# Measured delays between engines in a list scheduler, and VectorE's on-chip operations placed by GpSimd's ends

## The chip, the cores and the metric

The kernel runs on one core of one Trainium2 chip. A core has a matrix engine (TensorE, PE in the profile), a vector engine (VectorE, DVE), an activation engine (ScalarE, ACT), a general engine (GpSimd, POOL) and a queue engine (SyncE, SP) that issues the DMAs. Each runs its own instruction list in order, and they meet only through semaphores. SBUF is the on-chip memory; PSUM is the small memory that TensorE writes. The metric is device microseconds for the whole program; less is better.

## What is computed

Three blocks in a row: a linear attention with exponential features, a mixture of eight experts whose gates are normalized over rows and columns by turns, and one wide block with a sigmoid gate.

```python
def _attn_ref(q, k, v, omega):           # 4 x 8 heads x 576 tokens x 64, 128 features
    def phi(x):
        h = x @ omega.T - sum(x * x) / 2
        return exp(h - max(h)) / sqrt(m)
    kv = einsum('bhsm,bhsd->bhmd', phi(k), v)
    return (phi(q) @ kv) / (phi(q) @ phi(k).sum() + 1e-6)

def _moe_ref(x, w_gate, w1, w2):         # 2304 tokens x 512, 8 experts of 1024
    P = exp(logits - logits.max())       # then 8 rounds of row and column normalization
    for e in range(8):
        out += P[:, e:e + 1] * (maximum(x @ w1[e], 0) @ w2[e])

def _moe2_ref(x, w_in, w_out):           # 512 -> 2048 -> 512
    h = x @ w_in
    return (h * sigmoid(1.702 * h)) @ w_out
```

## The kernel before

The matrix products are made in float32 precision out of three products of rounded halves (a high part and a low part of each operand), and blocks of four are combined into seven products instead of eight by sums and differences of blocks, so that the other engines form many sums while TensorE multiplies. The 2304 tokens are cut into three groups of 768 (j = 0 to 2). The hidden features are taken two blocks of 256 at a time (c = 0 and 1), which makes 16 pairs for the experts and 4 for the last block. One pair on one token group is a **visit**; there are 60. A visit has an up part (`up_fast`, L1195, 84 matmuls of 384 columns), and a down part (`down_across`, L1349, 84 of 384 columns for the experts; `down`, L1386, 256 columns for the last block). The down part of one visit runs into the up part of the next.

In the up part the PSUM results are combined on VectorE (L1216), gated on VectorE (L1237: relu and gate in one operation), and turned into operands of the down part by `operand`: ScalarE rounds a tile into its high part (L1205, tiles named `h` with c, a number 0 to 6 and 0), and an engine subtracts it for the low part (names ending in 1). Where the source lies in PSUM, VectorE subtracts (L1216). Where it lies in the SBUF tile `ring`, `tt` (L426) records the subtraction at L429 for "VP": either VectorE or GpSimd, as the planner decides. The same helper makes the sums of weight blocks (`raw`), the low parts of the weights (`w1x`, `w2x`, GpSimd alone), sums in `ring`, and at the change from the experts to the last block the operands of the next input out of `acc` (`y_operands`, with high parts at L1046). PSUM results of the down part are added to `acc` on VectorE (L1367, L1412) or copied to another bank by ScalarE (L1361).

The weights of the last block come as 64-bit floats. Between about 440 and 1400 us, 32 pieces are converted (`double_piece`): six VectorE operations each (L1125 to L1141) on the SBUF tile `x2s`, then one on GpSimd (L1149).

Nothing of this is issued in the order of the source. Every operation is recorded in a `Plan` with the engine, a duration, what it reads and writes. `Plan.deadlines` goes back from TensorE's list and gives each operation a latest start; `Plan.run` then plays the program in time: at each moment each free engine takes, of its ready operations, the one with the earliest deadline. "VP" operations lie in a list that VectorE and GpSimd share, and "AV" operations (two PSUM copies of the attention stage, L582 and L689) in one that ScalarE and VectorE share. TensorE's main list is fixed. The order that comes out is the order in which instructions are issued, so the durations and delays in the planner set the order, and the hardware's semaphores the times.

The lines that the change touches are the planner's constants (L33 to L37), `add`, the choice of the next operation in `run` (L134 to L185), the duration formulas (L414 to L424) and `double_piece`.

## Time and profile before

| what | us |
|---|---|
| median of 3 runs (1969.64 to 1972.14) | 1970.06 |
| the profiled execution | 1969.8 |
| its span, first to last instruction | 1968.0 |
| TensorE busy | 1931.8 (98%) |
| VectorE busy | 1483.1 (75%) |
| GpSimd busy | 1265.6 (64%) |
| ScalarE busy | 1044.7 (53%) |
| attention stage, about | 0 to 165 |
| experts, about | 165 to 1600 |
| last block, about | 1600 to 1963 |

A line of a group in the profile reads: source line, engine, operation, tile written and tiles read, shape, count, then busy time, mean duration, and the idle time of its engine just before such instructions with what ended it. In a timeline, a bracket behind a row gives the idle time of that engine ahead of it and the instruction that ended it. Matmuls overlap in the array, so their durations (335 ns) are longer than their spacing; TensorE's pace is read from how many it starts in a stretch of time.

### The profile page before, as it was taken

To read this page: it belongs to the slowest core of one execution; us is meant where nothing else is said; L and a number is where in the kernel's file an instruction comes from. 1 tells how busy PE (TensorE), PEld (TensorE's weight loads), DVE (VectorE), ACT (ScalarE), POOL (GpSimd) and SP (SyncE) were. 2 spreads that over 40 slices of the span, in tenths; PEclk is the share of its full clock that TensorE was granted. 3 is DMA by queue.
4 is the path that set the end of the run, shared out by engine and by line. 5 is a ranking of instruction groups with operands and counts; after the bars stand their busy time and mean duration, and the time that the engine had idled before them with its cause. 6 is when DMAs were issued, how large, how long until landed. Compare 5 with 4: busy or idle time off the path is not lost.

```text
span 1968.0 us, 36376 instructions
## 1 busy us (share of the span) xinstructions
PE 1931.8 (98%) x12899; PEld 1888.0 (96%) x12899; DVE 1483.1 (75%) x2882; ACT 1044.7 (53%) x2393; POOL 1265.6 (64%) x1250
## 2 busy tenths in 40 slices
PE   9999999999999999999999999999999999999998
PEld 7788999999999999999999999999999989999998
DVE  7884377777788788888888797888776785656655
ACT  6885555445445355354445354444545576755653
POOL 5844284866658485766667485757656895847552
PEclk9999999999999999999999999999999999999999
DMA  9867465667677586677676685776676888745653
GB/s 171 215 180 244 151 229 218 224 243 250 230 261 258 214 291 239 232 269 257 221 280 241 220 301 206 253 274 228 235 259 214 293 298 320 264 179 202 238 211 120
DMA packets 259295, 464.07 MB, mean 236 GB/s; under 512 B 75288, under 2 KB 200104, under 8 KB 259112
## 3 DMA queue, kind: packets, MB, share of 16 engines
q1 hardware_dynamic: 259112, 461.74, 67.7%
q8 instruction: 102, 1.67, 0.3%
q14 instruction: 81, 0.66, 0.1%
HBM read 415.45 MB, written 46.21 MB: 235 GB/s over the span
## 4 chain that ended last, share of the span: by engine, by line
PE 78%; DVE 12%; ACT 3%; issue 3%; POOL 2%; DMA 1%; SPq 0%; DVEq 0%; ACTq 0%; POOLq 0%
PE bank L1195 35%; PE bank L1349 29%; PE bank L1386 8%; DVE ring L1216 2%; DVE bank L1237 2%; DVE h L1216 2%; PE bank L598 2%; DVE h L429 2%; DVE bank L1216 1%; ACT acc L637 1%; PE bank L576 1%; POOL h L429 1%; PE pair L704 1%; PE bank L684 1%; PE pair L654 1%
## 5 line engine op out<-in xcount | busy, mean ns | idle before, releaser
L1195 PE MATMUL bank<-xo,w1x 128*128 128x384 f32 x5040 | 913.4, 335 | 1.9 <-ACT ring L1205 1.3
L1195 PEld LDWEIGHTS bank<-xo,w1x 128*128 128x128 f32 x5040 | 875.4, 188 | 5.5 <-ACT bank L1205 2.5
L1349 PE MATMUL bank<-h,w2x 128*128 128x384 f32 x4032 | 734.4, 337 | 7.4 <-ACT bank L1361 3.0
L1349 PEld LDWEIGHTS bank<-h,w2x 128*128 128x128 f32 x4032 | 700.1, 188 | 19.5 <-ACT bank L1361 6.7
L429 POOL TENSOR_TENSOR h<-ring,h 128x384 fp32r<-128x384 f32 x350 | 375.1, 1087 | 152.4 <-ACT h L1205 130.3
L1367 DVE TENSOR_TENSOR acc<-bank,acc 128x384 f32<-128x384 f32 x552 | 282.5, 551 | 141.7 <-PE bank L1349 135.1
L1205 ACT ACTIVATE h<-ring 128x384 fp32r<-128x384 f32 x480 | 239.2, 529 | 152.7 <-DVE ring L1216 143.7
L1205 ACT ACTIVATE ring<-bank 128x384 f32<-128x384 f32 x480 | 235.4, 492 | 148.2 <-PE bank L1195 143.3
L429 POOL TENSOR_TENSOR w1x<-raw,w1x 128x768 fp32r<-128x768 f32 (+1 forms) x120 | 181.2, 1516 | 204.0 <-ACT w1x L1101 203.1
L1205 ACT ACTIVATE bank<-bank 128x384 f32<-128x384 f32 x216 | 103.1, 480 | 386.1 <-PE bank L1195 347.9
L429 POOL TENSOR_TENSOR raw<-raw 128x256 f32<-128x256 f32 x313 | 238.1, 784 | 58.3 <-DMA raw<-in_moe_w_dram 43.0
L1216 DVE TENSOR_TENSOR h<-bank,h 128x384 fp32r<-128x384 f32 x324 | 178.5, 551 | 114.4 <-ACT ring L1205 90.4
L1237 DVE SCALAR_TENSOR_TENSOR bank<-bank,x2s 128x384 f32<-128x384 f32 x336 | 183.9, 558 | 67.6 <-PE bank L1195 66.7
L1216 DVE TENSOR_TENSOR ring<-bank,ring 128x384 f32<-128x384 f32 x432 | 225.7, 547 | 8.5 <-ACT bank L1205 6.3
L429 POOL TENSOR_TENSOR ring<-ring 128x384 f32<-128x384 f32 x111 | 116.0, 1045 | 171.2 <-ACT ring L1205 122.3
L1205 ACT ACTIVATE h<-bank 128x384 fp32r<-128x384 f32 x360 | 176.3, 492 | 53.2 <-DVE bank L1237 38.4
L429 POOL TENSOR_TENSOR w2x<-raw,w2x 128x768 fp32r<-128x768 f32 (+1 forms) x120 | 182.8, 1535 | 23.8 <-ACT w2x L1101 23.3
L1386 PE MATMUL bank<-w2x,h 128*128 128x256 f32 x1512 | 186.6, 281 | 5.7 <-POOL w2x L429 2.4
L1386 PEld LDWEIGHTS bank<-w2x,h 128*128 128x128 f32 x1512 | 183.2, 189 | 8.0 <-POOL w2x L429 2.6
L1216 DVE TENSOR_TENSOR bank<-bank,ring 128x384 f32<-128x384 f32 x240 | 133.4, 558 | 14.2 <-PE bank L1195 12.4
L429 DVE TENSOR_TENSOR h<-ring,h 128x384 fp32r<-128x384 f32 x130 | 121.5, 948 | 4.0 <-ACT h L1205 1.9
L1101 ACT CAST w2x<-raw 128x768 fp32r<-128x768 f32 (+1 forms) x120 | 81.5, 694 | 56.3 <-POOL raw L429 51.4
(132 smaller groups left out, 1307.7 us busy)
## 6 DMA issues: line engine op xcount, KB each, us to landing
xo<-sx SPq DMA_DIRECT2D x413, 768.0 KB, 7.1
raw<-in_moe_w_dram SPq DMA_DIRECT2D x256, 128.0 KB, 4.4
x2s<-scr_g SPq DMA_DIRECT2D x90, 192.0 KB, 6.8
sx<-acc SPq DMA_DIRECT2D x46, 192.0 KB, 3.5
x2s<-in_moe_w_in_dram SPq DMA_DIRECT2D x16, 512.0 KB, 4.6
x2s<-in_moe_w_out_dram SPq DMA_DIRECT2D x16, 512.0 KB, 4.1
sx<-x2s SPq DMA_DIRECT2D x35, 192.0 KB, 3.9
sx<-xo SPq DMA_DIRECT2D x42, 128.0 KB, 2.9
```

The source lines that it names most:

```text
L429: lambda e: e.tensor_tensor(out=out(), in0=a(), in1=b(), op=op), r, w,
L576: nc.tensor.transpose(pt[:, i * P : (i + 1) * P], x[:, 2 * i : 2 * i + 2, :], ident)
L598: nc.tensor.matmul(pj[e][0][:, i * M : (i + 1) * M], xt[r, i * P : (i + 1) * P], om[r, :], start=True, stop=True, skip_group_check=True,)
L637: lambda h=h, pv=pv: nc.scalar.activation(f[:, h, :], pv[:, h // 2, :], AF.Exp, bias=nb[:, h : h + 1], scale=-1.0),
L1101: lambda e, a=a, b=b: nc.scalar.copy(T[w, c, 0][:, a:b], r[:, a:b]), raws, [(w, c, g, 0)],
L1195: nc.tensor.matmul(o(b), T["w1", c, a][:, slot, kk], T["xo"][x][:, y, kk], start=start and kk == 0 and n == 0, stop=kk == 1 and n == 2, sk ...
L1205: rec("ACT", act_us(Q), lambda e: nc.scalar.activation(out(), src(), f, **kw), r, w)
L1216: lambda e: e.tensor_tensor(out=out[0](), in0=a[0](), in1=b[0](), op=op), [a[1], b[1]], [out[1]],
L1237: lambda e: e.scalar_tensor_tensor(out=out[0](), in0=o(b), scalar=0.0, in1=T["G"][th], op0=ALU.max, op1=ALU.mult),
L1349: nc.tensor.matmul(bank[i][:, :Q], T["w2", c, y][:, slot, k * P : (k + 1) * P], T["h", c, a, x], start=s and m == 0, stop=c == 1 and m == ...
L1367: lambda e, i=i, q=q: e.tensor_tensor(out=q, in0=bank[i][:, :Q], in1=q, op=ALU.add), rd + [key], [key],
L1386: nc.tensor.matmul(bank[i][:, u], T["h", c, a, x][:, t * P : (t + 1) * P], T["w2", c, y][:, slot], start=s and m == 0, stop=c == 1 and m = ...
```

## The change

Five things are changed, all in the planner and its numbers.

1. One delay of 0.17 us from any engine to any other becomes a table by pair of engines (0.2 from TensorE to ScalarE or VectorE, 0.163 to TensorE, 0.035 between ScalarE and VectorE, 0.035 to 0.08 with GpSimd). The restart cost for TensorE goes.
2. The time by which an engine can start its next operation ahead of the end of the last becomes a number by engine (0.08, 0.1 and 0.04 us instead of 0.07).
3. Durations: a two-input SBUF operation of 384 columns is reckoned at 0.544 us on VectorE instead of 1.015, and at 1.017 us on GpSimd instead of 1.115. A conversion step is reckoned at 0.55 us instead of 1.07. A matmul of 384 columns is 0.1743 instead of 0.1735 us.
4. Operations whose operands lie on chip in SBUF (the VP ones and the six conversion steps) are marked `lock`. The planner lets such an operation on VectorE end no earlier than GpSimd's present operation plus its own time, and lets GpSimd start nothing before VectorE's marked operation is nearly through.
5. VectorE takes a marked operation only where GpSimd's operation ends within 0.5 us (`PATIENCE`), and not where GpSimd is free or about to be free (`RACE`) and has something else to take.

```diff
-    LAT = 0.17
+    LAT = {
+        ("PE", "ACT"): 0.2, ("PE", "DVE"): 0.2, ("ACT", "PE"): 0.163, ("DVE", "PE"): 0.163, ("POOL", "PE"): 0.163,
...
+    NEXT = {"DVE": 0.08, "ACT": 0.1, "POOL": 0.04}
+    LATER = 0.17
     BELOW = 2.5
     AHEAD = 3.0
-    LEAP = 0.07
-    RESTART = 0.1
+    MANY = 14
+    PATIENCE = 0.5
+    RACE = 0.13
...
+        o.lock = lock or eng == "VP"
...
-                    heappush(sets[o.eng], (o.late, o.n, o))
+                    heappush(sets["TIED" if o.eng == "DVE" and o.lock else o.eng], (o.late, o.n, o))
...
-            for e in ("X", "PE", "DVE", "POOL", "ACT", "SP"):
+            for e in ("X", "PE", "POOL", "DVE", "ACT", "SP"):
...
+                elif e == "DVE":
+                    both, wait = sets["VP"], pool_end - t
+                    free = min((h for h in (sets["DVE"], sets["AV"]) if h), key=lambda h: h[0], default=None)
+                    tied = sets["TIED"] or None
+                    if both and (both[0][0] - t + drift <= self.BELOW or len(both) >= self.MANY):
+                        if tied is None or both[0] < tied[0]:
+                            tied = both
+                    if tied is not None and wait > self.PATIENCE:
+                        tied = None
+                    if tied is not None and at["POOL"] <= t + self.RACE:
+                        if at["POOL"] > t + 1e-9 and (sets["POOL"] or len(both) > (tied is both)):
+                            tied = None
+                        elif any(x[0] <= t + self.RACE and x[2].eng in ("POOL", "VP") for x in soon):
+                            tied = None
+                    if tied is not None and free is not None and free[0] < tied[0]:
+                        tied = None
+                    h = tied if tied is not None else free
+                    if h is not None:
+                        o = heappop(h)[2]
...
-                    d = (o.dur[e] if isinstance(o.dur, dict) else o.dur) + rest
+                    d = o.dur[e] if isinstance(o.dur, dict) else o.dur
                     o.end = t + d
-                    at[e] = o.end if e in ("PE", "X") else o.end - self.LEAP
+                    if e == "DVE" and o.lock:
+                        o.end = max(o.end, pool_end + d - 0.125)
+                        hold = max(hold, o.end - 0.12)
+                    elif e == "POOL":
+                        o.end = pool_end = max(t, hold) + d
+                    at[e] = o.end - self.NEXT.get(e, 0.0)
...
-        return {"DVE": dve_us(n), "POOL": 0.27 + 0.0022 * n}
+        return {"DVE": 0.145 + 0.00104 * n, "POOL": 0.18 + 0.00218 * n}
...
-        us = 0.25 + 0.0016 * WIDE
+        us = 0.55
...
-            rec("DVE", us, s, R + W, W, due=at + 8.0 + 4.0 * i)
+            rec("DVE", us, s, R + W, W, due=at + 8.0 + 4.0 * i, lock=True)
```

What it does to the order is shown at two places. In the changed file lines from L429 on stand 27 lines lower (L429 is L456, L1216 is L1243, L1237 is L1264, L1367 is L1394).

First place: VectorE in the visit that begins at 951 us, from the middle of its up part on. `bank` tiles are PSUM, `h` tiles are operands of the down part, `ring` and `x2s` lie in SBUF. Before:

```order
L1216 TENSOR_TENSOR bank7_2526<-bank3_102,ring_69 128x384
L1216 TENSOR_TENSOR ring_69<-bank0_99,ring_69 128x384
L1237 SCALAR_TENSOR_TENSOR bank7_2526<-bank7_2526,x2s_75 128x384
L429 TENSOR_TENSOR h031_2375<-ring_69,h030_2374 128x384
L1216 TENSOR_TENSOR bank4_103<-bank4_103,ring_69 128x384
L1216 TENSOR_TENSOR h161_2395<-bank7_2526,h160_2394 128x384
```

The same place in the change:

```order
L1243 TENSOR_TENSOR bank7_2503<-bank3_102,ring_69 128x384
L1264 SCALAR_TENSOR_TENSOR bank7_2503<-bank7_2503,x2s_75 128x384
L1243 TENSOR_TENSOR bank4_103<-bank4_103,ring_69 128x384
L1243 TENSOR_TENSOR ring_69<-bank0_99,ring_69 128x384
L1243 TENSOR_TENSOR h161_2376<-bank7_2503,h160_2375 128x384
```

The subtraction for h031, with both operands in SBUF, has gone from VectorE. GpSimd at the same place, before (`w1x` is the low part of a weight block):

```order
L429 TENSOR_TENSOR ring_69<-ring_69 128x384
L429 TENSOR_TENSOR h021_2373<-ring_69,h020_2372 128x384
L429 TENSOR_TENSOR w1x_70<-raw1_68,w1x_70 128x512
L429 TENSOR_TENSOR h041_2377<-ring_69,h040_2376 128x384
L429 TENSOR_TENSOR h051_2379<-ring_69,h050_2378 128x384
```

and in the change:

```order
L456 TENSOR_TENSOR w1x_70<-raw0_67,w1x_70 128x512
L456 TENSOR_TENSOR h031_2356<-ring_69,h030_2355 128x384
L456 TENSOR_TENSOR h021_2354<-ring_69,h020_2353 128x384
L456 TENSOR_TENSOR ring_69<-ring_69 128x384
L456 TENSOR_TENSOR h041_2358<-ring_69,h040_2357 128x384
L456 TENSOR_TENSOR w1x_70<-raw1_68,w1x_70 128x512
L456 TENSOR_TENSOR h121_2368<-ring_69,h120_2367 128x384
L456 TENSOR_TENSOR h141_2372<-ring_69,h140_2371 128x384
L456 TENSOR_TENSOR h051_2360<-ring_69,h050_2359 128x384
```

GpSimd now makes h031, h121 and h141 too, which VectorE made before. It makes h031 ahead of h021 and `ring`, and `w1x` after h041.

Second place: GpSimd at the change from the experts to the last block, up to the first low part of the new down weights (`w2x`). Before:

```order
L429 TENSOR_TENSOR w1x_70<-raw1_68,w1x_70 128x768
L429 TENSOR_TENSOR w1x_70<-raw0_67,w1x_70 128x512
L429 TENSOR_TENSOR w1x_70<-raw1_68,w1x_70 128x512 x2
L429 TENSOR_TENSOR acc1_73<-acc1_73,x2s_75 128x384 x2
L429 TENSOR_TENSOR acc1_73<-acc1_73,acc0_72 128x384
L429 TENSOR_TENSOR ring_69<-ring_69 128x384
L429 TENSOR_TENSOR x2s_75<-x2s_75,acc1_73 128x384 x2
L429 TENSOR_TENSOR acc2_74<-acc2_74,acc1_73 128x384
L429 TENSOR_TENSOR raw0_67<-raw0_67 128x256
L429 TENSOR_TENSOR h031_2375<-ring_69,h030_2374 128x384
L429 TENSOR_TENSOR w2x_71<-raw0_67,w2x_71 128x768
```

In the change:

```order
L456 TENSOR_TENSOR ring_69<-ring_69 128x384
L456 TENSOR_TENSOR x2s_75<-x2s_75,acc1_73 128x384
L456 TENSOR_TENSOR acc2_74<-acc2_74,acc1_73 128x384
L456 TENSOR_TENSOR raw0_67<-raw0_67 128x256
L456 TENSOR_TENSOR raw1_68<-raw1_68 128x256
L456 TENSOR_TENSOR w2x_71<-raw0_67,w2x_71 128x768
```

The `w1x` rows have moved up, to before h041 of the last expert visit, and h031 no longer stands ahead of the first `w2x`.

## Rows read from the trace of the kernel before

**Rows 1.** The page, part 1: busy us (share of the span) x instructions.

```profile
PE 1931.8 (98%) x12899; PEld 1888.0 (96%) x12899; DVE 1483.1 (75%) x2882; ACT 1044.7 (53%) x2393; POOL 1265.6 (64%) x1250
```

**Rows 2.** Stretches: from:to us, length, busy us (x instructions) by engine, granted clock, DMA.

```profile
50.00:100.00 50.00, 44.51 (x723) 38.61 (x723) 42.02 (x101) 42.44 (x132) 40.68 (x63) 1.00 0.84 215
...
150.00:200.00 50.00, 45.69 (x325) 41.53 (x324) 22.36 (x45) 24.19 (x54) 21.70 (x27) 1.00 0.76 240
200.00:440.00 240.00, 239.52 (x1376) 233.46 (x1375) 165.40 (x337) 120.62 (x258) 154.89 (x146) 1.00 0.60 217
440.00:1400.00 960.00, 953.05 (x5437) 942.93 (x5437) 799.10 (x1486) 454.96 (x966) 629.19 (x584) 1.00 0.69 247
1400.00:1540.00 140.00, 140.00 (x807) 139.68 (x806) 105.05 (x199) 70.97 (x150) 92.75 (x89) 1.00 0.67 243
...
1600.00:1650.00 50.00, 44.13 (x278) 42.31 (x277) 36.03 (x56) 37.44 (x87) 42.10 (x35) 0.97 0.91 317
1650.00:1960.00 310.00, 308.93 (x2212) 307.03 (x2212) 183.03 (x386) 180.31 (x425) 172.48 (x164) 1.00 0.57 208
```

**Rows 3.** Waits of TensorE's weight loads: line <- releaser, us in total, times, longest.

```profile
PEld bank L1349 <- ACT bank L1361: 6.7, 12, 0.8
PEld bank L1349 <- DVE acc L1367: 4.6, 10, 0.7
PEld bank L1349 <- DVE h L1216: 4.3, 8, 0.6
...
PEld bank L1349 <- POOL h L429: 1.4, 3, 0.5
```

**Rows 4.** Timeline of 959 to 963 us: start, duration, engine, instruction, idle before.

```profile
959.44 1.29 POOL L429 TENSOR_TENSOR w1x<-raw,w1x 128x512 fp32r<-128x512 f32 x1 [0.25 <-ACT w1x L1101]
959.46 1.69 DVE L429 TENSOR_TENSOR h<-ring,h 128x384 fp32r<-128x384 f32 x1
...
961.07 0.55 DVE L1216 TENSOR_TENSOR bank<-bank,ring 128x384 f32<-128x384 f32 x1
961.54 0.54 DVE L1216 TENSOR_TENSOR h<-bank,h 128x384 fp32r<-128x384 f32 x1
...
962.13 1.58 PEld L1349 LDWEIGHTS bank<-h,w2x 128*128 128x128 f32 x9 [0.61 <-DVE h L1216]
```

**Rows 5.** Groups of VectorE instructions over the span: busy us, mean ns, idle before.

```profile
L1216 DVE TENSOR_TENSOR ring<-bank,ring 128x384 f32<-128x384 f32 x432 | 225.7, 547 | 8.5 <-ACT bank L1205 6.3 <-POOL h L429 0.5
...
L429 DVE TENSOR_TENSOR h<-ring,h 128x384 fp32r<-128x384 f32 x130 | 121.5, 948 | 4.0 <-ACT h L1205 1.9
...
L1129 DVE SCALAR_TENSOR_TENSOR x2s<-x2s 128x512 uint32<-128x512 uint32 x32 | 40.2, 1257 | 0.5
...
L1132 DVE TENSOR_SCALAR x2s<-x2s 128x512 uint32<-128x512 uint32 x32 | 17.6, 551 | 0.0
```

**Rows 6.** L429 alone in one stretch: length, VectorE busy (x), GpSimd busy (x).

```profile
440.00:1400.00 960.00, 61.39 (x70) 590.50 (x553) 1.00 0.69 247
```

**Rows 7.** Two conversion steps by line: shortest/median/longest ns, first and last start.

```profile
L1129 DVE SCALAR_TENSOR_TENSOR x2s<-x2s x32: 681/961/2385, 473.5 to 1393.9; 128x512 uint32<-128x512 uint32 x32
L1132 DVE TENSOR_SCALAR x2s<-x2s x32: 415/421/962, 474.1 to 1394.5; 128x512 uint32<-128x512 uint32 x32
```

**Rows 8.** Timeline of 1608 to 1617 us: TensorE's weight loads, and GpSimd.

```profile
1609.65 2.04 PEld L1195 LDWEIGHTS bank<-xo,w1x 128*128 128x128 f32 x12 [0.69 <-ACT ring L1205]
...
1614.10 0.19 PEld L1386 LDWEIGHTS bank<-w2x,h 128*128 128x128 f32 x1 [2.40 <-ACT w2x L1101]
...
1614.85 1.99 POOL L429 TENSOR_TENSOR w2x<-raw,w2x 128x768 fp32r<-128x768 f32 x1
...
1616.89 1.35 PEld L1386 LDWEIGHTS bank<-w2x,h 128*128 128x128 f32 x6 [2.61 <-POOL w2x L429]
```

**Rows 9.** A ScalarE group of the attention stage, up to 165 us.

```profile
L582 ACT ACTIVATE b<-bank 128x512 f32<-128x512 f32 x20 | 12.5, 624 | 17.7 <-PE bank L576 17.6
```

**Rows 10.** The longest wait of TensorE's matmuls: us in total, times, longest.

```profile
PE bank L598 <- ACT acc L637: 6.0, 8, 1.2
```

**Rows 11.** The page, part 5: GpSimd's largest group.

```profile
L429 POOL TENSOR_TENSOR h<-ring,h 128x384 fp32r<-128x384 f32 x350 | 375.1, 1087 | 152.4 <-ACT h L1205 130.3 <-PE bank L1195 11.3 <-DMA xo<-sx 6.3
```

47 lines of the change are left out of this document (22 added, 25 removed).

## Prediction, made before the changed kernel ran

> **What bounds the kernel now.** I read the page's shares first: TensorE is busy 98% of the span [rows 1], so a gain can only come from time that TensorE loses. Busy time hides part of the loss, since matmuls overlap and their ends are modelled, so the table of stretches comes next [rows 2]; the reader is to see two rows in it. From 1400 to 1540 us TensorE is busy all 140.00 us and starts 807 matmuls, nearly all of 384 columns: 140 / 807 = 0.1735 us each, its pace without waits. From 440 to 1400 it starts 5437, which at that pace is 943.3 us. So 16.7 of these 960 us are lost, 2.4 times the 6.95 us of idle that the row shows. The other losses: 200 to 440 us, 240 - 1376 x 0.1735 = 1.3 us; 1600 to 1650, 5.87 us idle and a mean granted clock of 0.97 (part of it at 1.2 instead of 2.4 GHz), which is 0.03 x 50 = 1.5 us more, in all 7.4; 1650 to 1960, 1.07 idle, by the same factor of 2.4 some 2.6 us. In the attention stage TensorE is idle 5.49 us between 50 and 100, and 4.31 us between 150 and 200 [rows 2]. I take these as waits on ScalarE and on the path of x, which the change hardly addresses.
>
> Then the question is who TensorE waits for in the middle. Its loads for the down part wait 6.7 us on ScalarE's bank copies, 4.6 on VectorE's additions to `acc`, 4.3 on VectorE's low parts out of PSUM, and only 1.4 on GpSimd [rows 3]. So VectorE's chain is late, directly or through ScalarE, which copies what VectorE has freed. The timeline at 959 us shows why [rows 4]: VectorE begins h031 at 959.46, just after GpSimd began a 1.29 us operation at 959.44, and ends at 961.15. It takes 1.69 us. The PSUM operations behind it, 0.55 us each, stand in line; h161 comes at 961.54, and TensorE's load at 962.13 has been idle for 0.61 us on it. In the mean such a subtraction takes VectorE 948 ns where an operation of the same size with a PSUM operand takes 547 [rows 5]. The conversion steps show the same: line L1129 takes 681 ns at best, 1257 in the mean and 2385 at worst, L1132 415, 551 and 962 [rows 5, 7]. VectorE waits for GpSimd with its operation at the head of its list.
>
> **The change part by part.** *New prices and delays.* They issue nothing. TensorE's list keeps its order but for 11 of 11,996 rows, so TensorE's own work is unchanged, and I cost this at nothing by itself.
>
> *VectorE's on-chip operations.* Over the program VectorE does 87 instead of 165 of the L429 operations and GpSimd 1163 instead of 1085. What counts is where they stand. I counted VectorE's order from h001, with which a visit's chain begins, to the last PSUM operation of its up part, for the 33 visits in 440 to 1400 us. In this front part stood 62 of L429 and 70 conversion steps; now 7 and 45. The others stand behind it, among the additions to `acc`, as in the two lists for the visit at 951 us. Price before: L429 61.39 / 70 = 0.877 us [rows 6], 62 x 0.877 = 54.4 us. The six steps sum to 159.9 us in 192 operations between the first and last of rows 5, 0.833 us each, and 70 x 0.833 = 58.3. Together 112.7 us. Price after: alone an L429 operation is bounded by the PSUM row of 0.547 [rows 5], a step by the mean of the two shortest, (0.681 + 0.415) / 2 = 0.548 [rows 7]. To each I add half of the 0.5 us that the new rule lets it wait. 7 x 0.80 + 45 x 0.80 = 41.6 us; bounds 28.5 us (no wait) and 43.6 us (today's prices). So 71.1 of 112.7 us, 63%, leave the chain, and I take the same share of the 16.7 us: 10.5 us. The upper bound is all 16.7, as from 1400 to 1540, where L429 stands in the front part and no conversion does. The lower: only the waits that end on VectorE itself shorten, (4.6 + 4.3) of (6.7 + 4.6 + 4.3), 57% [rows 3], giving 6.0.
>
> *The early visits and the last block.* The same rule brings the L429 operations in the front part from 12 down to 2 in the eight visits from 200 to 440 us, and from 17 to 3 in the last eleven visits. I take 1.0 of 1.3 us and 1.5 of 2.6; bounds 0 and all.
>
> *The change of blocks.* At 1614.10 and 1616.89 TensorE's loads had been idle 2.40 us on the first rounded weights and 2.61 on their low part, which GpSimd began at 1614.85 and needed 1.99 us for [rows 8]. In the second pair of lists the old up weights (`w1x`) are made earlier, so `raw` comes free earlier for the new loads on SP's queue, and h031 no longer stands ahead of `w2x`. VectorE keeps its share here (33 instead of 26 L429 operations in the two visits around it). One row of 1.09 us [rows 11] out of the way and an earlier `raw` could take most of both waits, and with them the slow clock of 0.97 that follows. I take 4 of the 7.4 us; bounds 0 and 7.4.
>
> *Attention.* Eight PSUM copies move from VectorE to ScalarE: 8 x 0.624 = 5.0 us [rows 9], on an engine that TensorE waits for 6.0 us already [rows 10]. VectorE gets as much free. I take 0, with -2 to +4.
>
> *GpSimd's new load.* 78 operations of 1.087 us [rows 11] are 85 us on an engine that is busy 64% [rows 1]. They hide in its idle time, 36% of the span; where one comes late TensorE waits 1.4 / 3 = 0.47 us [rows 3]. I take four such, 2 us; bounds 0 and 6.
>
> *A rule against it.* GpSimd and VectorE take turns in rows 4: while one works on chip the other stands. The Trainium skill ("Perfetto Trace Analysis", Optimizing Scalar/DVE Operations) says that the two share an SBUF read port, so moving operations between them might not help; by it alone the sum would be 0. The rows agree on the turns, but the operations queued behind the blocked one read PSUM, and two of these took 0.55 us each with GpSimd at work [rows 4].
>
> **The sum.** 10.5 + 1.0 + 1.5 + 4 + 0 - 2 = 15.0 us. 1969.8 (the profiled execution; span 1968.0 and 1.8 around it) less 15.0 is 1954.8; the median lies 0.26 above the profiled execution, so 1955. All upper bounds together give 16.7 + 1.3 + 2.6 + 7.4 + 2 = 30, so 1940; all lower ones 6.0 - 4 - 6 = -4, so 1974.
>
> **The rivals.** *The chain is late by its own length.* If PSUM operations and their order make VectorE late, not the on-chip ones, the gain is the lower bound in the middle and little else: 6.0 + 1 - 2 = 5, 1965. For it: the largest single sum in rows 3 is ScalarE's. Against: 1400 to 1540 us has the same PSUM work and no loss.
>
> *Turns are merely swapped.* VectorE holds fewer turns, but each moved operation takes 1.087 instead of about 0.55 us of them, 78 x 0.54 = 42 us more in all. If GpSimd's operands come late by as much as VectorE's come early, nothing is gained: 1966.1 to 1974. For it: the rule above. Against: GpSimd has idle time in every stretch of rows 2.
>
> *GpSimd becomes late, and it is slower.* h121 and h141 now stand in GpSimd's list behind weight parts of 1.29 us and more [rows 4], with one engine to make them. If TensorE waits 0.47 us [rows 3] for one operand in each of 60 visits, that is 28 us against the 17 of the sum without its last term: 1981. It decides from 17 / 0.47, some 36 late operands. Against: three in the whole trace now.
>
> **How the numbers follow.** The forecast, 1940 to 1962, 0.63; own length, 1962 to 1966, 0.15; swapped, 0.13; slower, 1974 to 1985, 0.09. About 0.2%, 4 us, can be told from no change here: faster 0.78, same 0.13, slower 0.09. The range from 1944 to 1969 leaves out the slower case, half of the swapped one and the top of the forecast, under 0.2 in all.
>
> **What would show it.** Right: L429 on VectorE near 0.7 us in the mean instead of 0.9, the conversion steps near 0.7; loss in 440 to 1400 us near 6; the waits of L1349 loads on VectorE and ScalarE halved; one instead of two long waits near 1614 us. Wrong: those waits keep their size (own length), or the row of GpSimd's h in rows 3 grows beyond 10 us (late GpSimd), or the loss before 165 us grows by more than 4 us.

## The result and the profile after

The changed kernel takes 1983.59 us in the median (1980.91 to 1991.65, five executions) against 1969.64 (1969.15 to 1972.14) of the kernel before in the same comparison: the ratio is 1.0078, with a 95% interval from 1.0051 to 1.0105. It is slower by 14 us, where 15 us less was predicted. The profiled execution is the longest, 1991.65 us (span 1989.9). In the lines below all that was L429 or later has moved by 27: L429 is L456, L1195 is L1222, L1205 is L1232, L1216 is L1243, L1349 is L1376, L1361 is L1388, L1386 is L1413. The files of the other kernels are of other lengths, so their lines have other numbers for the same operations.

The stretches of the profile after, as in [rows 2] (length, busy us by engine with the count, granted clock, DMA):

```profile
200.00:440.00 240.00, 231.12 (x1302) 224.43 (x1301) 154.34 (x303) 113.24 (x246) 152.81 (x149) 0.98 0.55 199
440.00:1400.00 960.00, 954.80 (x5447) 944.22 (x5447) 766.25 (x1448) 457.12 (x971) 664.33 (x631) 1.00 0.70 251
1600.00:1650.00 50.00, 40.82 (x247) 38.96 (x246) 36.14 (x62) 31.71 (x72) 38.58 (x34) 0.93 0.84 282
1650.00:1960.00 310.00, 306.97 (x2165) 303.07 (x2165) 162.67 (x354) 182.03 (x423) 188.02 (x185) 1.00 0.62 228
```

By the prediction's own measure the middle loses 960 - 5447 x 0.1735 = 14.9 us, where [rows 2] gave 16.7: 1.8 us won, not 10.5. Even this is no sure gain of the new order. Four other profiles, of h131_pool and raw_due below, have the same order in this stretch but no long stall ahead of it; they start 5424 to 5435 matmuls there, a loss of 17.0 to 18.9 us (1.5 to 1.6 us of it wait for one long operation told of below). The stretches around it lost: 1302 instead of 1376 matmuls from 200 to 440, and 247 instead of 278 from 1600 to 1650.

TensorE runs the same 12,899 matmuls, in nearly the same order, in every kernel here. So the start of one and the same matmul can be compared: the table gives how many us later (or, with a minus, earlier) it starts than in the profile of the kernel before, for the matmul that starts there at the time at the head of the column. A step between two columns is what that stretch cost. The second profile of the change repeats the steps of the first to 0.2 us, but for the one to 177 us (6.6 instead of 4.4 won). The kernels are explained below.

| kernel | 100 | 177 | 280 | 400 | 430 | 1000 | 1500 | 1585 | 1640 | 1950 |
|---|---|---|---|---|---|---|---|---|---|---|
| the change | -4.7 | -4.4 | 3.3 | 4.7 | 12.7 | 11.1 | 11.5 | 14.7 | 18.7 | 21.7 |
| the change, second profile | -7.2 | -6.6 | 1.1 | 2.5 | 10.4 | 9.0 | 9.0 | 12.2 | 16.3 | 19.5 |
| h131_pool | -6.3 | -5.3 | 0.3 | 1.7 | 1.0 | -0.6 | 3.2 | 6.5 | 10.8 | 14.0 |
| undo_rule | -6.6 | -6.1 | -0.3 | 1.7 | 1.0 | 31.8 | 53.4 | 58.1 | 62.2 | 65.9 |
| undo_delays | -0.7 | -1.3 | 0.0 | -1.1 | 6.7 | 6.2 | 7.2 | 11.8 | 13.4 | 12.1 |
| undo_prices | -6.5 | -7.6 | -6.6 | -6.1 | -6.8 | 6.4 | 15.5 | 16.0 | 26.9 | 27.5 |
| gate_first | -6.8 | -6.2 | -0.9 | -0.6 | -1.3 | -7.1 | -8.4 | -5.2 | 0.4 | 3.9 |
| no_share | -4.9 | -4.6 | 3.3 | 3.4 | 2.7 | 4.9 | 5.2 | 5.2 | 23.0 | 24.9 |
| raw_due | -6.1 | -5.5 | 0.6 | 2.0 | 1.3 | 0.0 | 2.6 | 5.6 | 4.2 | 8.2 |
| attention_only | -4.9 | -6.8 | -6.1 | -6.1 | -6.3 | -5.5 | -5.2 | -5.2 | -5.2 | -4.8 |
| middle_alone | 0.0 | 0.2 | 0.2 | 0.2 | 0.2 | 2.5 | 8.5 | 10.8 | 15.4 | 15.4 |
| middle_gate | -0.3 | -0.3 | -0.2 | -0.2 | -0.2 | -2.3 | -3.2 | -1.5 | -1.6 | -1.7 |
| both_parts | -6.3 | -8.8 | -6.0 | -6.0 | -6.2 | -9.5 | -10.0 | -9.5 | -8.9 | -9.0 |
| both_raw | -6.8 | -9.0 | -7.6 | -7.0 | -7.3 | -10.5 | -11.0 | -7.2 | -6.8 | -6.8 |

The change's own row is an account of its 21.7 us: 4.4 won in the attention stage, 7.7 lost from 177 to 280, 1.4 to 400, 8.0 lost within 30 us after 400, 1.2 won to 1500, 7.2 lost at the change of blocks (1500 to 1640), 3.0 in the last block. Four places are followed here; the cause of the loss in the last block stays open.

**Early visits.** Two waits of TensorE's loads, and what VectorE did before the second (timeline: start, duration, idle before):

```profile
177.19 0.69 DVE L820 TENSOR_TENSOR acc<-bank,acc 128x512 fp32r<-128x512 f32 x1 [2.02 <-DMA sx<-acc]
177.93 0.42 PEld L799 LDWEIGHTS bank<-ident,x2s 128*128 128x128 f32 x4 [2.62 <-DVE acc L820]
...
266.59 1.57 DVE L982 TENSOR_SCALAR sig<-sig 128x18 f32<-128x18 f32 x1
268.50 1.02 DVE L985 TENSOR_TENSOR sig<-sig 128x144 f32<-128x144 f32 x1
270.02 0.30 PEld L995 LDWEIGHTS bank<-sig 128*128 128x128 f32 x2 [2.01 <-DVE sig L989]
```

At 177 us VectorE may not overwrite a piece of `acc` before its store has left; at 270 us the chain that normalizes the gates ends late. After both, TensorE runs at 1.2 instead of 2.4 GHz for a while (a granted clock of 0.51 and 0.57 in the first two rows here; the last two are behind the stalls at 410 and 1628):

```profile
179.00:186.00 7.00, 6.00 (x21) 5.20 (x20) 2.59 (x5) 3.03 (x7) 3.88 (x4) 0.51 1.07 400
271.00:275.00 4.00, 4.00 (x16) 4.00 (x15) 2.96 (x9) 1.38 (x3) 1.80 (x3) 0.57 0.45 159
416.00:423.00 7.00, 6.82 (x25) 6.57 (x26) 4.03 (x9) 0.00 (x0) 0.00 (x0) 0.60 0.01 4
1633.00:1640.00 7.00, 4.32 (x15) 4.03 (x16) 2.25 (x5) 4.22 (x9) 5.71 (x4) 0.52 0.71 210
```

The lower clock cost 0.49 x 7 = 3.4 us behind the wait of 2.62 us, 0.43 x 4 = 1.7 behind the one of 2.01, and 0.40 x 7 = 2.8 behind the stall of 6.21 us below.

**One VectorE operation of 8.83 us.** Timeline of VectorE, GpSimd and TensorE's loads after 404 us:

```profile
404.74 4.97 POOL L456 TENSOR_TENSOR h<-ring,h 128x384 fp32r<-128x384 f32 x5
407.30 8.83 DVE L456 TENSOR_TENSOR h<-ring,h 128x384 fp32r<-128x384 f32 x1
409.64 4.17 POOL L456 TENSOR_TENSOR raw<-raw 128x256 f32<-128x256 f32 x6
413.73 1.97 POOL L456 TENSOR_TENSOR acc<-acc,x2s 128x384 f32<-128x384 f32 x2
416.18 1.14 PEld L1376 LDWEIGHTS bank<-h,w2x 128*128 128x128 f32 x4 [6.21 <-DVE h L456]
```

h131 begins on VectorE at 407.30, in the third of five GpSimd operations, and ends at 416.13, 0.43 us after a run of 13 GpSimd operations without a gap (404.74 to 415.70). GpSimd works through all of them while it stands. TensorE's load waits 6.21 us.

**The up part.** Waits of TensorE's weight loads from 440 to 1400 us, before and then after:

```profile
PEld bank L1349 <- ACT bank L1361: 6.1, 10, 0.8
PEld bank L1349 <- DVE h L1216: 4.1, 7, 0.6
PEld bank L1349 <- DVE acc L1367: 2.6, 5, 0.5
PEld bank L1195 <- ACT bank L1205: 2.3, 5, 0.5
PEld bank L1349 <- POOL h L429: 1.4, 3, 0.5
```

```profile
PEld bank L1222 <- ACT ring L1232: 6.2, 9, 1.2
PEld bank L1376 <- ACT bank L1388: 5.3, 16, 0.5
PEld bank L1376 <- DVE acc L1394: 2.7, 7, 0.5
```

The down part's loads waited 6.1 + 4.1 + 2.6 + 1.4 = 14.2 us before and 8.0 after. The up part's waited 2.3 and now 6.2, on copies that ScalarE makes into `ring`. One of these, at 1176 us, with VectorE and ScalarE ahead of it:

```profile
1171.34 1.44 DVE L1162 SCALAR_TENSOR_TENSOR x2s<-x2s 128x512 f32<-128x512 uint32 x1
...
1173.75 1.03 DVE L1264 SCALAR_TENSOR_TENSOR bank<-bank,x2s 128x384 f32<-128x384 f32 x2
1174.35 0.95 ACT L1232 ACTIVATE h<-bank 128x384 fp32r<-128x384 f32 x2 [1.63 <-DVE bank L1264]
...
1176.12 0.47 PEld L1222 LDWEIGHTS bank<-xo,w1x 128*128 128x128 f32 x3 [1.20 <-ACT ring L1232]
```

A conversion step (L1162, 1.44 us) stands ahead of two of VectorE's PSUM operations and the gate L1264; ScalarE waits 1.63 us for the gate, and frees TensorE's bank 1.20 us late. It is the pattern of nearly all these waits: in eight of the nine, 5.7 of the 6.2 us, a conversion step is among the three VectorE operations ahead of the gate that ScalarE waits for.

**The change of blocks.** SP's queue and TensorE's loads:

```profile
1614.87 3.70 SPq L460 DMA_DIRECT2D sx<-x2s  x3
1618.62 2.86 SPq L460 DMA_DIRECT2D raw<-scr_out  x5
...
1627.71 0.42 SPq L460 DMA_DIRECT2D raw<-scr_out  x1
...
1629.17 0.49 SPq L460 DMA_DIRECT2D raw<-scr_out  x1
...
1634.26 0.29 PEld L1413 LDWEIGHTS bank<-w2x,h 128*128 128x128 f32 x1 [5.98 <-ACT w2x L1128]
...
1636.26 0.93 PEld L1413 LDWEIGHTS bank<-w2x,h 128*128 128x128 f32 x4 [1.71 <-POOL w2x L456]
```

Both long waits of [rows 8] are still there, 5.98 and 1.71 us instead of 2.40 and 2.61. GpSimd had made its last `w1x` out of the old `raw` by 1604.42, yet the new loads come 14 to 25 us later, behind stores (`sx`) that wait for operands of the next input.

### The profile page after: what moved, and what is told of

Same layout as the page of the kernel before. It is cut to its first block, busy times and chain, and to the rows that moved or that the text cites. A ratio compares the mean times of both kernels' runs of the same rounds, so it can differ in the third digit from the quotient of the medians.

```text
span 1989.9 us, 36279 instructions
## 1 busy us (share of the span) xinstructions
PE 1941.6 (98%) x12899; PEld 1893.6 (95%) x12899; DVE 1424.5 (72%) x2796; ACT 1050.9 (53%) x2401; POOL 1321.3 (66%) x1328
## 4 chain that ended last, share of the span: by engine, by line
PE 72%; DVE 12%; ACT 7%; DMA 3%; issue 3%; POOL 2%; SPq 1%; DVEq 0%; POOLq 0%; ACTq 0%
PE bank L1222 30%; PE bank L1376 29%; PE bank L1413 8%; DVE bank L1264 2%; DVE ring L1243 2%; ACT h L1232 2%; DVE h L1243 2%; DVE bank L1243 1%; ACT ring L1232 1%; PE bank L625 1%; ACT acc L664 1%; DMA sx<-acc 1%; POOL raw L456 1%; DMA raw<-in_moe_w_dram 1%; ACT bank L1232 1%
## 5 line engine op out<-in xcount | busy, mean ns | idle before, releaser
L1222 PE MATMUL bank<-xo,w1x 128*128 128x384 f32 x5040 | 918.9, 337 | 8.7 <-ACT ring L1232 8.2
L1222 PEld LDWEIGHTS bank<-xo,w1x 128*128 128x128 f32 x5040 | 876.0, 188 | 16.8 <-ACT ring L1232 13.3
L1376 PE MATMUL bank<-h,w2x 128*128 128x384 f32 x4032 | 737.1, 339 | 11.3 <-DVE h L456 8.2
L1376 PEld LDWEIGHTS bank<-h,w2x 128*128 128x128 f32 x4032 | 704.8, 189 | 21.5 <-DVE h L456 9.5
L456 POOL TENSOR_TENSOR h<-ring,h 128x384 fp32r<-128x384 f32 x424 | 438.7, 1058 | 79.7 <-ACT h L1232 76.3
L1394 DVE TENSOR_TENSOR acc<-bank,acc 128x384 f32<-128x384 f32 x552 | 289.5, 553 | 170.8 <-PE bank L1376 162.3
L1232 ACT ACTIVATE bank<-bank 128x384 f32<-128x384 f32 x216 | 103.8, 480 | 501.0 <-PE bank L1222 471.2
L1232 ACT ACTIVATE ring<-bank 128x384 f32<-128x384 f32 x480 | 230.0, 490 | 119.3 <-PE bank L1222 108.8
L456 POOL TENSOR_TENSOR w1x<-raw,w1x 128x768 fp32r<-128x768 f32 (+1 forms) x120 | 178.4, 1491 | 151.7 <-ACT w1x L1128 151.0
L1243 DVE TENSOR_TENSOR h<-bank,h 128x384 fp32r<-128x384 f32 x324 | 179.4, 554 | 128.7 <-ACT ring L1232 100.3
L456 POOL TENSOR_TENSOR raw<-raw 128x256 f32<-128x256 f32 x313 | 232.7, 767 | 57.8 <-DMA raw<-in_moe_w_dram 43.0
L1232 ACT ACTIVATE h<-ring 128x384 fp32r<-128x384 f32 x480 | 236.0, 526 | 62.3 <-DVE ring L1243 52.8
L1264 DVE SCALAR_TENSOR_TENSOR bank<-bank,x2s 128x384 f32<-128x384 f32 x336 | 188.4, 562 | 75.4 <-PE bank L1222 69.7
L1243 DVE TENSOR_TENSOR ring<-bank,ring 128x384 f32<-128x384 f32 x432 | 223.3, 550 | 22.3 <-ACT bank L1232 18.7
L1232 ACT ACTIVATE h<-bank 128x384 fp32r<-128x384 f32 x360 | 176.7, 492 | 98.3 <-DVE bank L1264 81.0
L456 POOL TENSOR_TENSOR ring<-ring 128x384 f32<-128x384 f32 x118 | 121.3, 1028 | 158.3 <-ACT ring L1232 101.8
L456 POOL TENSOR_TENSOR w2x<-raw,w2x 128x768 fp32r<-128x768 f32 (+1 forms) x120 | 180.9, 1517 | 25.9 <-ACT w2x L1128 23.0
L1413 PE MATMUL bank<-w2x,h 128*128 128x256 f32 x1512 | 187.6, 281 | 8.2 <-ACT w2x L1128 5.7
L1413 PEld LDWEIGHTS bank<-w2x,h 128*128 128x128 f32 x1512 | 183.8, 189 | 11.0 <-ACT w2x L1128 6.0
L1243 DVE TENSOR_TENSOR bank<-bank,ring 128x384 f32<-128x384 f32 x240 | 133.7, 558 | 9.5 <-PE bank L1222 7.9
L1176 POOL TENSOR_TENSOR x2s<-x2s 128x512 f32<-128x512 f32 x32 | 41.4, 1293 | 117.3 <-DVE x2s L1168 113.5
L1439 DVE TENSOR_TENSOR acc<-bank,acc 128x256 f32<-128x256 f32 x180 | 69.1, 421 | 62.4 <-PE bank L1413 55.7
```

Of the source, the lines that this page charges most:

```text
L456: lambda e: e.tensor_tensor(out=out(), in0=a(), in1=b(), op=op), r, w,
L1176: lambda e: e.tensor_tensor(out=mf(), in0=mf(), in1=af(), op=ALU.add), W, W, due=at + 32.0,
L1222: nc.tensor.matmul(o(b), T["w1", c, a][:, slot, kk], T["xo"][x][:, y, kk], start=start and kk == 0 and n == 0, stop=kk == 1 and n == 2, sk ...
L1232: rec("ACT", act_us(Q), lambda e: nc.scalar.activation(out(), src(), f, **kw), r, w)
L1243: lambda e: e.tensor_tensor(out=out[0](), in0=a[0](), in1=b[0](), op=op), [a[1], b[1]], [out[1]],
L1264: lambda e: e.scalar_tensor_tensor(out=out[0](), in0=o(b), scalar=0.0, in1=T["G"][th], op0=ALU.max, op1=ALU.mult),
```

## The experiments

**Which part of the change costs?** Three kernels undo one part each.

undo_rule (the new prices and delays stay):

```diff
-            for e in ("X", "PE", "POOL", "DVE", "ACT", "SP"):
+            for e in ("X", "PE", "DVE", "POOL", "ACT", "SP"):
...
-                    if e == "DVE" and o.lock:
-                        o.end = max(o.end, pool_end + d - 0.125)
-                        hold = max(hold, o.end - 0.12)
...
-                    if tied is not None and wait > self.PATIENCE:
-                        tied = None
+                elif e in ("DVE", "POOL"):
+                    own, both = sets[e], sets["VP"]
...
```

> The change with one part undone: VectorE and GpSimd choose their operations by the old rule again; the new delays and the new prices stay (109 instead of 87 on-chip L456 operations on VectorE; before 165). Theory 'the rule costs' (VectorE's on-chip operations now stand where they hold up what follows): time falls to before's 1970 or below, and the waits of the up part's loads on ScalarE's ring copies (13.3 us in the change, 2.4 before) fall to about 3. Rival 'the delays cost' (orders packed so tight by the new delays that any late operation reaches TensorE): the rule only helped, so without it the middle loses at least the 16.7 us of before, on top of the change's later stretches: 1981 to 1990. Rival 'any new order costs, wherever it falls': no pattern, with the change of blocks (13 us of loss in the change, 7 before) moving by several us.

2036.4 us (ratio 1.0333, interval 1.0320 to 1.0347), slower than under any of the theories. The loads of 440 to 1400 us:

```profile
PEld bank L1203 <- ACT ring L1213: 19.8, 15, 3.7
PEld bank L1357 <- DVE acc L1375: 19.1, 13, 2.6
```

undo_delays:

```diff
-    LAT = { ...
+    LAT = LATER = 0.17
...
-                        x = o.end - self.NEXT.get(e, 0.0)
...
+                    s.ready = max(s.ready, o.end + ((0.0 if e == "PE" else 0.05) if s.eng == e else self.LAT))
```

> The change with one part undone: the single delay of 0.17 us, the old start-ahead and the restart cost are back, and 0.1735 us for a matmul; the rule and the new prices stay (130 on-chip operations on VectorE). 'The delays cost': TensorE's waits in the up part on ring copies go (8 us of its time) and the loss of 7.5 us between 177 and 322 us goes, while the 4 us won in the attention stage go too: about 1981 - 8 - 7.5 + 4 = 1970. 'The rule costs': the time stays near 1981. 'Any new order': anything from 1965 to 1985, with another place for the largest stall.

1982.7 us (1.0061, 1.0049 to 1.0073).

undo_prices (the small changes to the prices of ScalarE's and PSUM operations go back too, not shown):

```diff
-        return {"DVE": 0.145 + 0.00104 * n, "POOL": 0.18 + 0.00218 * n}
+        return {"DVE": 0.17 + 0.0022 * n, "POOL": 0.27 + 0.0022 * n}
...
-        us = 0.55
+        us = 0.25 + 0.0016 * WIDE
```

> The change with one part undone: VectorE's on-chip operation is reckoned at 1.015 us and a conversion step at 1.07 us again; the new delays and the rule stay (159 on-chip operations on VectorE, nearly the 165 of before). If the prices bring the harm (the planner takes VectorE for free when it is not, and packs the up part), the ring waits fall from 13.3 us to below 5 and the time to 1970 or less. If the rule or the delays bring it, the time stays above 1978. By 'any new order' the sign can't be told.

1997.9 us (1.0136, 1.0123 to 1.0149). Loads of 440 to 1400 us:

```profile
PEld bank L1376 <- DVE h L456: 16.5, 15, 1.8
```

So "the rule costs" falls: without it the middle loses 960 - 5163 x 0.1735 = 64 us. The planner reckons a subtraction for `h` on VectorE at 0.544 us wherever it stands, and in this profile it took 0.859 us in the mean; that this is the reason is likely, not shown. The prices alone do not bring the harm either. Rule and prices belong together; beside the new delays, each alone is worse than both. The delays are where the attention gain comes from (-1.3 without them at 177 us, -4.4 to -7.6 with them), and in the change that gain is handed back by 280 us. The loss from 177 to 280 us needs the new delays and the new prices together: it is 7.7 us in the change, 1.3 without the delays and 1.0 without the prices. The loss in the last block is gone in these two as well (-1.3 and 0.6). No part undone gives before's time, so the question turned to places.

**The operation of 8.83 us.** h131_pool moves that one instruction:

```diff
         for e, o in plan.run():
+            if e == "DVE" and o.keys == (("h", 1, 3, 1),) and 404.0 < o.start < 406.0:
+                e = "POOL"
```

> The change with one instruction moved: the subtraction for h131 that took 8.83 us on VectorE at 407 us goes to GpSimd's list, between h121 and h141; nothing else differs. Theory 'starved in some executions': that operation alone makes the difference between the change's executions at 1981 and at 1990 to 1992 (6.05 us of waiting and 6.8 us at half the clock, 3.4 us, make 9.5), so now all executions lie at 1981 plus or minus 1.5, and the profile has no stall over 2 us between 272 and 1590. Rival 'the place is not special': executions at 1990 still occur, with a long VectorE operation elsewhere.

1983.22 us (1982.26 to 1990.09, six executions; 1.0074, 1.0059 to 1.0090). The 8 us after 400 us are gone from the table (1.7 to 1.0). But two of the six executions still took 1990, and the profiled one has an operation of 4.10 us elsewhere. The expectation holds for the place and fails for the whole spread. Second profiles of the change and of undo_delays:

> The changed kernel itself once more, for a second profile. Five executions took 1980.9 to 1991.7; the profiled one, 1991.65, had h131 at 407 us in VectorE for 8.83 us. 'Starved in some executions': if this one takes under 1985, h131 takes under 1.5 us and no VectorE on-chip operation takes over 5; if over 1988, one takes over 5 us. 'Something else varies': the time changes by over 5 us without such an operation.

> The change with the old delays once more. Its profile had VectorE operations of 7.99 us at 402 and 6.79 us at 1576, yet its five executions lay within 2.6 us. If being starved is decided by the order alone, the same two operations take 6 to 8 us again and the time is 1981 to 1985; if by chance in each execution, at least one of them takes under 2.5 us and the time is 5 to 8 us shorter.

They took 1989.55 and 1982.72 us. The operations in question, from the timelines of the change's second profile, of undo_delays and its second profile (two each), and of h131_pool:

```profile
405.14 8.88 DVE L456 TENSOR_TENSOR h<-ring,h 128x384 fp32r<-128x384 f32 x1
```

```profile
402.24 7.99 DVE L450 TENSOR_TENSOR h<-ring,h 128x384 fp32r<-128x384 f32 x1
...
1576.20 6.79 DVE L450 TENSOR_TENSOR x2s<-acc 128x384 f32<-128x384 f32 x1
```

```profile
403.18 8.00 DVE L450 TENSOR_TENSOR h<-ring,h 128x384 fp32r<-128x384 f32 x1
...
1576.03 6.79 DVE L450 TENSOR_TENSOR x2s<-acc 128x384 f32<-128x384 f32 x1
```

```profile
1083.66 4.10 DVE L456 TENSOR_TENSOR h<-ring,h 128x384 fp32r<-128x384 f32 x1
```

The same operations are long again, to within 0.05 us: the order of a program decides where this can happen. In undo_delays the long operations are in both profiles, and its executions lie together; they stand where its row of the table goes up by 7.8 us (400 to 430) and 4.6 us (1500 to 1585). The change has h131 long in both profiles, of 1989.55 and 1991.65 us. None of its executions of 1981 to 1984 was profiled; the profiles of raw_due below show the same place without the long operation.

**Without shared operations on VectorE.** no_share:

```diff
-                    if both and (both[0][0] - t + drift <= self.BELOW or len(both) >= self.MANY):
+                    if both and t < 300.0 and (both[0][0] - t + drift <= self.BELOW or len(both) >= self.MANY):
...
-                        if slack < flex.dur["POOL"] - flex.dur["DVE"] and at["DVE"] < t + 0.5:
+                        if t < 300.0 and slack < flex.dur["POOL"] - flex.dur["DVE"] and at["DVE"] < t + 0.5:
```

> The change with VectorE taking no shared on-chip operation after the planner's 300 us: all L456 operations of the experts and the last block go to GpSimd (87 more), VectorE keeps the conversion steps. Theory 'starved in some executions' (two-input operations of VectorE that stand behind a gapless run of GpSimd): no VectorE operation above 2.5 us after 330 us and no executions 7 us or more above the others. What it costs, if GpSimd becomes late: waits of TensorE's loads on GpSimd's h above 5 us in 440 to 1400 (0 in the change), time 1985 to 1995. If GpSimd has the room: 1978 to 1982.

1994.46 us (1.0117, 1.0104 to 1.0130), four executions within 2.2 us. In the middle GpSimd has the room (its h cost TensorE's loads 1.1 us there, and the step from 430 to 1500 us is 2.5), at the change of blocks not: 17.8 us are lost from 1585 to 1640 against 4.0 in the change, with 6.3 us of waits on GpSimd's h and 11.5 on the weights' operands (7.7 on `w2x`, 3.8 on `w1x`). One conversion step took 3.21 us, so the bound of 2.5 us did not hold, but no execution stood apart.

**The up part.** gate_first keeps VectorE free where one of its PSUM operations is about to become ready:

```diff
+                    if tied is not None and any(
+                        x[0] <= t + 0.5 and x[2].eng == "DVE" and not x[2].lock for x in soon
+                    ):
+                        tied = None
                     if tied is not None and free is not None and free[0] < tied[0]:
                         tied = None
```

> The change with one condition more: VectorE takes no on-chip operation where one of its PSUM operations becomes ready within 0.5 us (65 instead of 87 on-chip L456 operations on VectorE; the 192 conversion steps stay but stand elsewhere). Theory: the change moved on-chip operations from in front of the down part's chain to in front of the gate in the up part, so that ScalarE's ring copies come late (4.8 us of TensorE's time in 440 to 1400). Then those waits fall below 1.5 us, the loss of that stretch from 14.9 to about 10, and the time from 1982 to about 1976. Rival 'no slack': the operations put off come late elsewhere, the loss stays at 14 to 16 us, and the time at 1980 to 1985.

1973.99 us (1.0015, 1.0006 to 1.0024). The middle, and its loads' waits:

```profile
440.00:1400.00 960.00, 957.86 (x5482) 951.23 (x5481) 757.72 (x1443) 464.23 (x985) 671.93 (x641) 1.00 0.69 250
```

```profile
PEld bank L1226 <- ACT ring L1236: 4.9, 12, 0.8
PEld bank L1380 <- ACT bank L1392: 0.9, 3, 0.4
...
PEld bank L1380 <- DVE acc L1398: 0.5, 1, 0.5
```

The loss is 960 - 5482 x 0.1735 = 8.9 us, 7.8 less than before, and 7.1 us are won between 430 and 1500. The theory's total holds, one of its numbers does not: the ring waits fell only from 6.2 to 4.9, while the down part's fell from 8.0 to 1.4. Of the ring waits those with a conversion step ahead of the gate fell from 5.7 to 2.0 us (four of now twelve); the other 2.9 us have other chains behind them. So on-chip operations that start just before a PSUM operation hurt both parts, and the greater part of the gain is in the down part, where the theory did not put it. The 9.6 us between the two medians are not all the middle's: the long h131 is absent in this profile.

**The change of blocks.** raw_due:

```diff
-                        prepare(pi + 1, "w2", c, c)
+                        prepare(pi + 1, "w2", c, c, **({"due": plan.clock - 30.0} if l == 0 and pairs[pi + 1][0] else {}))
```

> The change with one number more: at the change of blocks the loads of the new down weights into raw are due 30 us earlier, so that they are planned 20 to 30 us earlier on SP's queue, ahead of the stores that wait for y operands. Theory 'raw is late behind waiting stores': the two stalls on w2x (5.83 and 1.88 us in the change's profile, with 6.8 us at half the clock behind them) go, the loss around the change of blocks falls from 13 to 5 us, the time from 1982 to about 1973. Rival 'the x path decides': the stall moves to the loads of the up part or to operands h at the same place, and less than 2 us is gained.

1986.19 us in the median, but in two kinds: 1978.03 in the profiled execution, 1983.59 to 1987.61 in the five others (1.0068, 1.0054 to 1.0082). In the median nothing is gained on the change. The profile loses 1.6 us from 1500 to 1640, where h131_pool, the change without the long operation, loses 7.6. The waits from 1580 to 1650 us, first of h131_pool, then of raw_due:

```profile
PEld bank L1413 <- ACT w2x L1128: 6.0, 1, 6.0
PEld bank L1376 <- DVE h L456: 3.3, 3, 1.9
...
PEld bank L1413 <- POOL w2x L456: 1.7, 1, 1.7
```

```profile
PEld bank L1222 <- ACT ring L1232: 2.9, 1, 2.9
PEld bank L1376 <- DVE h L456: 2.3, 2, 1.7
PEld bank L1222 <- DMA xo<-sx: 2.1, 2, 1.5
```

The w2x waits are gone and smaller ones on the path of x come in. To see an execution of the other kind, two more profiles of it were taken:

> The kernel with the earlier loads of raw once more, for a profile of one of its longer executions: five of six took 1983.6 to 1987.6 us, the profiled one 1978.0. Theory 'starved in some executions': the profile of a longer one shows one VectorE on-chip operation of 6 to 9 us behind a run of GpSimd operations without a gap, most likely h131 at about 405 us, and a stall of TensorE of 3 to 6 us on it; nothing else differs by more than 1 us. Rival 'something else varies' (the loads, the clock alone): no such operation, and the difference lies at several places.

> The kernel with the earlier loads of raw for a third profile: its executions stand at 1976 to 1978 and at 1983.6 to 1987.6, and the two profiled so far were of the first kind, with VectorE operations of at most 4.13 us. 'Starved in some executions': if this one takes over 1983, one VectorE on-chip operation takes over 6 us. 'Something else varies': none does.

They took 1976.07 and 1975.35 us: both of the short kind, so what the long kind holds was not seen. They lose 1.7 and 0.9 us from 1500 to 1640, as the first did, against 7.2 and 7.3 in the change's two profiles.

The three profiles show something else. Up to 1528 us raw_due issues the same operations in the same order as the change on every engine and on SP's queue. h131 is on VectorE again, behind the same run of GpSimd operations (first profile; compare 404.74 and 407.30 above):

```profile
402.05 5.30 POOL L456 TENSOR_TENSOR h<-ring,h 128x384 fp32r<-128x384 f32 x5
404.62 0.86 DVE L456 TENSOR_TENSOR h<-ring,h 128x384 fp32r<-128x384 f32 x1
```

It begins 2.57 us into the five GpSimd operations (2.56 in the change) and takes 0.86 us, 0.85 in the other two profiles, where the change's profiles have 8.83 and 8.88. So the order alone does not decide whether the operation is held up: with one and the same order it was in executions of 1990 and 1992 us, and was not in three of 1975 to 1978. That the long executions of the change and of raw_due are those with a long h131 fits, and is not shown for raw_due. The operation of 4.10 us in h131_pool is in all three (4.13, 4.07 and 4.12) and in neither profile of the change.

**The winning part alone.** attention_only is the kernel before with the new delays in the planner's first 165 us:

```diff
+    FIRST = 165.0
...
+                    if t <= self.FIRST:
+                        x = -self.NEXT.get(e, 0.0) if s.eng == e else self.EARLY.get((e, "DVE" if s.eng in ("VP", "AV") else s.eng), 0.1)
```

> The kernel before with one part of the change alone: the table of delays and the start-ahead by engine hold in the planner's first 165 us, everything later is planned with the old numbers and the old rule. Where the change's two kin with the new delays stood 6 to 7.6 us ahead of the kernel before at 177 us, this should stand 7 us ahead there. Theory 'the gain of the attention stage is real and lost only by what follows': it is kept, 1963. Rival 'x comes no earlier': it is handed back between 177 and 280 us, where the change lost 7.7 us, and the time is 1969 to 1971.

1966.5 us (0.9977, 0.9968 to 0.9986). It is 6.8 us ahead at 177 and 6.1 at 280: kept, 5 us in the end. So the rival falls, and what handed the gain back in the change lies in what it plans after 165 us.

**The middle alone.** The two kernels below plan with the whole change while the planner's clock is between 430 and 1490 us and as before elsewhere; middle_gate has gate_first's condition too.

```diff
+            new = self.FROM <= t < self.TO
+            quick = new or t <= self.FIRST
...
+                elif new and e == "DVE":
...
+                    if new:
+                        d = getattr(d, "new", d)
```

> The kernel before with the whole change (delays, prices, rule) in force only while the planner's clock is between 430 and 1490 us; the attention stage, the early visits, the change of blocks and the last block are planned as before. Theory 'the change wins in the middle only what its up part gives back': the loss in 440 to 1400 is 12 to 15 us (before 15 to 17), with ring waits in place of the waits on VectorE's h; the time is 1967 to 1970. Rival 'the middle gain was there and is lost elsewhere': 1958 to 1962.

> As the kernel with the change in the middle alone, plus the condition that VectorE takes no on-chip operation where one of its PSUM operations becomes ready within 0.5 us. Theory: what the change lacked in the middle is this condition; the loss in 440 to 1400 falls to about 7 us, as in the run with the condition on the whole change, 8 to 9 us less than before: 1961 to 1963. Rival 'an order of luck': 1966 to 1972.

middle_alone takes 1981.62 us (1.0063, 1.0051 to 1.0076), and loses 960 - 5394 x 0.1735 = 24 us in the middle, worse than both theories. Its down part waits:

```profile
PEld bank L1416 <- ACT bank L1428: 16.1, 31, 0.7
```

middle_gate takes 1968.84 us (0.9998, 0.9989 to 1.0006), no difference from the kernel before, which is what its rival forecast; it has 960 - 5461 x 0.1735 = 12.5 us lost in the middle of its profiled execution (1967.68). So the same rules, started from another state at 430 us, give 14.9 to 18.9 or 24 us without the condition and 8.9 or 12.5 with it. The condition wins in both surroundings; how much is not a property of the rule.

**Both parts together.** both_parts has FIRST = 165.0 and middle_gate's middle:

> The kernel before with the two parts that won: the table of delays in the first 165 us, and the change with the condition between 430 and 1490 us; the rest planned as before. If the two gains add up, 5.3 us from the attention stage and 8 to 9 from the middle: 1957. If the second is tied to the times at which the first ends (another place of the loads and stores), 1962 to 1966.

1959.99 us (1959.38 to 1961.07; 0.9949, 0.9936 to 0.9963): less than both kernels, 9.7 us less than the kernel before in this comparison, between the two expected times. 6.2 us stand at 430, 3.8 more at 1500, so the second part gives less than the 8 to 9 us expected. With the earlier loads of raw on top:

> The kernel with the two parts that won, plus the loads of raw at the change of blocks due 30 us earlier, as in the run on the whole change (where the stretch from 1585 to 1640 us lost 1.4 us less to 4 us more than before, instead of 4 to 7 more). Theory 'raw is late behind waiting stores' holds for before's order too: of the 2.25 and 2.68 us of waiting on w2x and the 1.7 us at half the clock there, 4 us go: 1956. Rival 'before's order is bound by the x path there': the stall moves to operands of the up part, 1958 to 1962.

1963.35 us in the median of five executions (1962.26 to 1965.43; 0.9957, 0.9945 to 0.9970); a sixth took 9016.85 us, for a reason that no trace shows, and is left out. The interval overlaps that of both_parts, so no difference between the two is shown. The w2x waits go here too, but in the profiles 4.2 us are lost from 1500 to 1640 against 1.1 in both_parts, on VectorE's banks and h and ScalarE's ring copies. The theory's 1956 fails, and the stall moves as the rival said, though the time lies above its range: in this order a late raw is one of several chains of nearly one length around the change of blocks.

## Why the prediction was wrong

- **The middle, 10.5 us.** 1.8 us were won in the profiled execution, below the lower bound of 6.0, and nothing in the four profiles of the same order without the long stall. The down part's chain was found right: its waits fell from 14.2 to 8.0 us, and nothing waits for GpSimd's h there any more. The sizes of the operations were right too: VectorE's L456 took 25.61 / 32 = 0.80 us (0.877 before, 0.80 expected), the six conversion steps 134.0 / 180 = 0.74 (0.833; 0.80 expected). The step that failed is the share: 63% of VectorE's on-chip time leaving "the front part" was taken as 63% of the loss. The front part was counted as one stretch from h001 to the last PSUM operation, and 45 of 70 conversion steps stayed in it; where they stand among the PSUM operations did not enter the sum. Some stand just ahead of a gate, and the up part's wait, 2.3 us before, took back 3.9 of the 6.2 won. With the condition of gate_first the loss is 8.9 us, 7.8 less than before: a gain near the forecast size was to be had, but not by the share. A smaller slip: the waits of [rows 3], which the prediction reads as the middle's, are of the whole span; from 440 to 1400 us they are 6.1, 2.6 and 4.1.
- **Early visits and last block, gains of 1.0 and 1.5.** Both were losses, 9.1 us from 177 to 400 and 3.0 from 1640. The prediction scaled the front part's count and didn't ask what else the new order moves. In the early visits these were the store of a piece of `acc` and the chain that normalizes the gates; for the last block it stays open.
- **The change of blocks, a gain of 4.** A loss of 7.2. "An earlier raw" was right as to when raw is free, and wrong as to the loads: SP's queue was named and not followed. They stood behind waiting stores. raw_due shows that this holds most of the change's loss there (0.9 to 1.7 us are left), both_raw that it isn't the only chain.
- **Attention, 0 (-2 to +4).** A gain of 4.4 to 6.6 us, where the prediction allowed 2 less to 4 more. The moved copies were costed on ScalarE, and the delays that rearrange the rest were costed at nothing. undo_delays shows that the gain comes with the delays; but without them the eight copies go back to VectorE too, so the two are not told apart.
- **GpSimd's load, a loss of 2.** Not seen in the middle, right in kind at the change of blocks only when all operations go there (no_share).
- **A term that was missing.** The longest VectorE operation in [rows 7] is 2.39 us, and that was taken as the worst. 8 us lie in one that is longer.
- **The rivals.** "GpSimd becomes late" gave 1981, near the result, by a mechanism that didn't occur: that is luck. None of the rivals contained a wait in the up part or the places outside the middle.

Open: what the longer executions of h131_pool and raw_due hold, what loses 3 us in the last block, and what decides, in one and the same order, whether VectorE loses its turn.

## What to carry to other kernels

When a scheduler's numbers change, read its new order at the stage borders and in every queue that waits in order (stores ahead of loads), not only where the loss is now; the gain here was a few us in one place and the losses in four others. Two changes that look like separate corrections can be one: truer prices without the rule that makes them true cost about 50 us more than both. An operation that can be held up should not start just before one that others wait for; one look-ahead condition took 6 us off the middle, more than the rule and the prices did there. Parts that win are best put in alone. And one profile of a program whose executions differ shows one kind of them: the operation of 8.83 us would have passed for a property of the order.
